# Block-sparse attention and a Sinkhorn mixture of experts on one core: how a weight's largest entry is spread over the partitions, how raw weights are loaded, and the planned order that follows

## The chip, the core and the metric

The kernel runs on one core of a Trainium2 chip. A core has five engines that run side by side, each in the order of its own program: TensorE (PE in the profile, with its weight loads as PEld), VectorE (DVE), ScalarE (ACT), GpSimd (POOL) and SyncE (SP), which here only issues DMA transfers. Matmul results lie in PSUM, in eight banks; everything else on the chip lies in SBUF, 128 partitions wide. The metric is device time of one execution in microseconds, measured on the chip. The median of three runs before the change is 2163.59 us (2163.19 to 2164.69).

## The reference

Four batches of eight heads with 768 positions and a head size of 64 go through attention with a block mask. The result is a matrix x of 3072 rows and 512 columns, which goes through eight experts. Each expert's output is weighted per row by a Sinkhorn-normalised gate. Cut to what matters:

```python
scores = np.where(mask, scale * (q @ k.T), -1e9)        # per batch and head, 768 x 768
attn = softmax(scores)
x = (attn @ v) -> 3072 x 512
P = sinkhorn(exp(x @ w_gate), 8 rounds)                 # 3072 x 8
for e in range(8):
    h = np.maximum(x @ w1[e], 0.0)                      # w1[e]: 512 x 1024
    ye = h @ w2[e]                                      # w2[e]: 1024 x 512
    out += P[:, e:e + 1] * ye
```

## The kernel before, in words

**Two phases.** The first 419 us of the profile are mostly attention, with gating beside its end. The rest is the experts: a loop over 32 steps, i = 4 e + b for expert e and batch b. Each step has a stage 1 (x times w1, then the maximum with zero) and a stage 2 (h times w2, then the weighted addition to the output).

**Products.** Both multiplications use Strassen's scheme: seven products of half-size blocks instead of eight, each f32 operand split into a high and a low f16 part, three matmuls per product. Stage 1 runs matmuls of 128x384 ("outer" products, L1580) and of 128x192 ("inner" ones, whose blocks are split once more, L1609) into five PSUM banks, p_0 to p_4. Stage 2 runs matmuls of 128x256 (L1932) into three banks, y_0 to y_2. DVE reads the p banks and combines them (L1553, L1646, L1662, L1684, L1840, L1848 and others write pair, u or h), and adds each y bank to the output sums acc (L1971, weighted by a tile named spare). A bank can be written again once DVE or ACT has read it.

**Weights.** The weights of an expert come as f32 from DRAM: `load_w` (L418, DMA at L422) brings the whole of w1[e] or w2[e], 2048 KB, into one tile r. Then the scale of that weight is worked out: eight absolute maxima on ACT (`magnitude`), one maximum over them on DVE (`whole`, L439), which leaves one number per partition in ma_w. `spread` (PE, L358) transposes that column through the identity matrix into a bank of stage 1, so that each partition sees all 128 numbers. `power` (DVE, L445 to L452) takes their maximum and turns it into a power-of-two scale sw and its inverse iw. With the scale, each of the seven blocks of the weight is split: the high part on ACT (L1334), the low part on DVE (L1339). Blocks that are sums or differences of raw blocks are made on POOL first (L1322), partly in place in the raw tile. The results are w2p_0 to w2p_6 for w2; for w1 they lie in the areas arena, attic and loft. These areas hold the blocks of x too, which are reloaded for each step (L473, L1487). From the scales of w1 and w2 the token weights of the expert are made (DVE, L1454 to L1458), the last of them named spare.

**Swap.** The w2p tiles exist once, so w2p of the next expert can be split only when stage 2 of this expert's last batch has used it. This part of the program, around the border of two experts, is called the swap below. There are seven of them, into e=1 to e=7, every 214 us or so. For e=0 the same jobs run before the first step.

**Order.** Every one of these pieces is a job of a plan (`Plan`, L129 to L288): it has an engine, an estimated duration, jobs it depends on, and for some a bank that it takes (`take`), gives back (`drop`) or holds. A list scheduler places the jobs, and the kernel pins each engine's program to that order. So a changed dependency or duration in a job moves others on all engines. DMAs on SP are jobs too; SP waits in its order before it issues each.

Of the kernel before, what the change touches and what calls it, by code (L numbers as in the profile page):

```python
# [9 lines left out]
F32 = mybir.dt.float32  # L10
# [6 lines left out]
ALU = mybir.AluOpType  # L17
# [3 lines left out]
P = 128  # L21
# [277 lines left out]
def tile_sparse_attention_moe(  # L299
# [116 lines left out]
    wr = {}  # L416

    def load_w(which, e):  # L418
        src, n, w = (w1, KD, FF) if which == 1 else (w2, KF, DM)
        t = raw.tile([P, KD * FF], F32, tag="r", name=f"r{which}_{e}")  # L420
        t = t.rearrange("p (c f) -> p c f", f=w)
        nc.sync.dma_start(out=t, in_=src[e].rearrange("(c p) f -> p c f", p=P))  # L422
        wr[which] = t

    def scale_steps(which, e, vector=nc.vector, scalar=nc.scalar):
# [27 lines left out]

        return [lambda k=k: part(k) for k in range(n)], whole, spread, power

# [137 lines left out]
    with ExitStack() as actx:  # L593
# [543 lines left out]
    def spare(n):  # L1137
# [151 lines left out]
    last_s3 = [()]  # L1289
    raw_free = [()]  # L1290
    pwe = {}

    def raw_load(which, e):
        return plan.dma(lambda: load_w(which, e), 2048, raw_free[0])

    def scale_jobs(which, e, loaded):
        cell = {}

        def make():
            cell["steps"] = scale_steps(which, e)  # L1300

        parts = []
        last = job({"-": 0.0}, make, (loaded,))
        for k in range(8):
            last = job({"ACT": 0.81}, lambda k=k: cell["steps"][0][k](), (last,))
            parts.append(last)
        whole = job({"DVE": 0.16}, lambda: cell["steps"][1](), parts)
        bk = hold("s1", ordered=False)

        def spread():  # L1310
            spread_bank[0] = lambda nm: bk.tile
            cell["steps"][2]()

        pe = job({"PE": 0.3}, spread, (whole,), take=(bk,), lag=2.0)
        power = job({"DVE": 1.2}, lambda: cell["steps"][3](), (pe,), drop=(bk,), rush=True)
        scaled[which, e] = power
        return parts, power
# [13 lines left out]
    def split_jobs(which, e, dst, src, deps):  # L1331
        s = lambda: wr["s", which]
# [4 lines left out]
        lo = job(  # L1337
            {"DVE": 1.29},
            lambda: nc.vector.scalar_tensor_tensor(  # L1339
                out=dst[:, 1], in0=src(), scalar=s(), in1=dst[:, 0], op0=ALU.mult, op1=ALU.subtract  # L1340
            ),
            (hi,), port=True,
        )
        return [hi, lo]

    def fetch_w1(e):
# [6 lines left out]

        loaded = job({"-": 0.0}, views, (loaded,) + tuple(last_s3[0]))
        parts, power = scale_jobs(1, e, loaded)
        g = lambda k: (lambda: a[k])
        q00, q10, q01, q11, s3 = (g(k) for k in ((0, 0), (1, 0), (0, 1), (1, 1), "s3"))
        base = tuple(parts)
        d_s3 = tts(s3, q00, q10, KH, base, 1.27)
        d_s1 = tts(q10, q10, q11, KH, tuple(d_s3), 1.27, ALU.add)  # L1360
        out = {}
# [5 lines left out]
        def inner(p, src, deps):  # L1367
# [36 lines left out]
        put(4, q10, d_s1)  # L1404
        last_s3[0] = tuple(out[5])
        raw_free[0] = tuple(x for p in out for x in out[p])
        split_done[1, e] = out

    def fetch_w2(e, loaded=None, done=None):
# [7 lines left out]

        if e == 0 or loaded is None:
            if loaded is None:
                loaded = raw_load(2, e)  # L1420
            start = job({"-": 0.0}, views, (loaded,) + tuple(last_s3[0]))
            parts, _ = scale_jobs(2, e, start)
# [705 lines left out]
```

## Time and profile before

| | before |
|---|---|
| median of three runs | 2163.59 us |
| profiled execution, its own time | 2163.22 us |
| its span in the profile | 2161.4 us |
| PE busy | 2113.7 us |
| DVE busy | 1778.1 us |
| ACT busy | 1363.3 us |
| POOL busy | 1170.3 us |

The span runs from the first to the last recorded instruction; the profiled execution's own time is 1.8 us longer. In the rows of the profile, "L1609 PE MATMUL p<-loft 128x192" is a matmul of line 1609 that writes a p bank from weights in loft; "x6" is a count; "[1.00 <-DVE pair L1662]" says that the engine stood idle for 1.00 us before it, until an instruction of line 1662 on DVE, which writes a tile pair, had ended. SPq is SP's queue of DMA issues.

### The profile page before, as it was taken

How to read it: one execution, taken by the hardware profiler on the slowest of the kernel's cores; microseconds unless marked ns; L12 is line 12 of the kernel's file. 1: busy time of each engine (PE TensorE's matmuls, PEld its weight loads, DVE VectorE, ACT ScalarE, POOL GpSimd, SP SyncE). 2: the span in 40 equal slices, each digit the busy share in tenths (PEclk: the TensorE clock that was granted, in tenths of full speed). 3: DMA queues.
4: the chain of work that ended last, by engine and by line, in shares of the span. 5: the costliest groups of instructions: out<-in, count | busy, mean ns of one | idle time of the engine just before them, and what ended most of it. 6: DMA issues, size and time to landing. Idle time of an engine off the chain costs nothing.

```text
span 2161.4 us, 51347 instructions
## 1 busy us (share of the span) xinstructions
PE 2113.7 (98%) x20620; PEld 1707.3 (79%) x20620; DVE 1778.1 (82%) x3240; ACT 1363.3 (63%) x2593; POOL 1170.3 (54%) x1336
## 2 busy tenths in 40 slices
PE   6999999999999999999999999999999999999999
PEld 4777776667777778788888888888888888888887
DVE  8878888688788878777988888888878987888776
ACT  4788888786567666655565556655655565556442
POOL 5556768465245547544665466446554564556323
PEclk9999999999999999999999999999999999999999
DMA  7667866432454644554354444544554445454421
GB/s 173 142 134 165 211 132 140 146 113 96 138 182 152 218 158 134 195 177 144 135 182 169 152 140 164 193 140 146 172 178 140 159 159 179 140 178 148 140 96 67
DMA packets 229412, 331.04 MB, mean 153 GB/s; under 512 B 135452, under 2 KB 153908, under 8 KB 229172
## 3 DMA queue, kind: packets, MB, share of 16 engines
q1 hardware_dynamic: 228608, 327.73, 49.6%
q8 instruction: 161, 2.64, 0.5%
q14 instruction: 79, 0.65, 0.1%
q10 hardware_dynamic: 564, 0.03, 0.0%
HBM read 228.62 MB, written 67.63 MB: 137 GB/s over the span
## 4 chain that ended last, share of the span: by engine, by line
PE 91%; DVE 6%; DMA 1%; issue 1%; ACT 1%; POOL 0%; SPq 0%; DVEq 0%; ACTq 0%; POOLq 0%
PE y L1932 39%; PE p L1580 23%; PE p L1609 15%; PE u L964 4%; PE t L902 2%; PE t L899 2%; PE m L866 2%; PE m L869 2%; DVE top L875 1%; DMA qt<-qs 1%; PE u L995 0%; DVE acc L1971 0%; DVE w2p L1339 0%; DVE pl L917 0%; DVE h L1815 0%
## 5 line engine op out<-in xcount | busy, mean ns | idle before, releaser
L1932 PE MATMUL y<-w2p,h 128*128 128x256 f16 x8064 | 969.3, 273 | 4.0 <-DVE w2p L1339 2.7
L1932 PEld LDWEIGHTS <-h 128*128 128x128 f16 x8064 | 785.4, 98 | 123.0 <-issue 3.7
L1798 POOL TENSOR_TENSOR h<-pair,h 128x384 f16<-128x384 f32 x413 | 414.7, 1016 | 489.9 <-ACT h L1809 429.7
L1971 DVE SCALAR_TENSOR_TENSOR acc<-y,spare,acc 128x256 f32<-128x256 f32 (+1 forms) x588 | 303.5, 518 | 151.5 <-PE y L1932 148.0
L1809 ACT ACTIVATE h<-pair 128x384 f16<-128x384 f32 x640 | 314.8, 516 | 138.9 <-DVE pair L1840 51.2
L1580 PE MATMUL p<-arena 128*128 128x384 f16 x1728 | 323.1, 326 | 1.4 <-DVE pair L1553 1.4
L1794 ACT ACTIVATE pair<-pair 128x384 f32<-128x384 f32 x384 | 194.9, 518 | 191.3 <-DVE pair L1553 161.8
L1553 DVE SCALAR_TENSOR_TENSOR pair<-p,pair 128x384 f32<-128x384 f32 x384 | 212.6, 555 | 93.6 <-PE p L1580 89.9
L1580 PEld LDWEIGHTS <-arena 128*128 128x128 f16 x1728 | 166.7, 98 | 83.5 <-issue 1.8
L875 DVE TENSOR_REDUCE top<-m 128x1 f32<-128x768 f32 x192 | 181.8, 951 | 48.5 <-PE m L869 47.7
L1609 PEld LDWEIGHTS <-loft 128*128 128x128 f16 x2304 | 198.8, 98 | 26.8 <-issue 11.1
L907 ACT ACTIVATE pe<-t,qk 128x768 int32<-128x768 f32 x192 | 172.3, 899 | 70.3 <-PE t L902 61.9
L1580 PE MATMUL p<-attic 128*128 128x384 f16 x1152 | 214.3, 326 | 0.0
L1840 POOL TENSOR_TENSOR pair<-pair,pair 128x384 f32<-128x384 f32 x120 | 128.3, 1076 | 106.6 <-DVE pair L1840 82.9
L1609 PE MATMUL p<-loft 128*128 128x192 f16 x1728 | 176.7, 246 | 8.5 <-DVE pair L1662 7.1
L1580 PEld LDWEIGHTS <-attic 128*128 128x128 f16 x1344 | 130.6, 98 | 66.8
L1798 POOL TENSOR_TENSOR h<-u,h 128x384 f16<-128x384 f32 x121 | 117.1, 975 | 119.4 <-ACT h L1809 77.1
L1562 ACT ACTIVATE u<-p 128x384 f32<-128x384 f32 x216 | 105.5, 488 | 103.7 <-PE p L1609 97.7
L1562 ACT ACTIVATE pair<-p 128x384 f32<-128x384 f32 x168 | 82.1, 490 | 113.0 <-PE p L1609 63.5
L1322 POOL TENSOR_TENSOR r<-r 128x256 f32<-128x256 f32 (+1 forms) x150 | 125.7, 850 | 39.2 <-DVE attic L1339 29.2
L866 PE MATMUL m<-kt,qt 128*128 128x512 f16 (+1 forms) x384 | 127.7, 333 | 10.0 <-DMA kt<-ks 6.6
L921 POOL TENSOR_SCALAR pl<-pe 128x768 f16<-128x768 uint16 x112 | 96.3, 863 | 71.7 <-ACT pe L907 69.4
(235 smaller groups left out, 3769.4 us busy)
## 6 DMA issues: line engine op xcount, KB each, us to landing
arena<-xd SPq DMA_DIRECT2D x128, 384.0 KB, 3.3
accd<-acc SPq DMA_DIRECT2D x56, 768.0 KB, 4.2
acc<-accd SPq DMA_DIRECT2D x56, 768.0 KB, 5.3
attic<-xd SPq DMA_DIRECT2D x96, 384.0 KB, 3.3
loft<-xsd SPq DMA_DIRECT2D x96, 384.0 KB, 4.9
r<-in_moe_w_dram SPq DMA_DIRECT2D x16, 2048.0 KB, 9.0
xd<-loft SPq DMA_DIRECT2D x28, 384.0 KB, 3.0
arena<-in_q_dram SPq DMA_DIRECT2D x16, 384.0 KB, 4.1
```

The costliest lines, as they stand in the source:

```text
L866: nc.tensor.matmul(sc[:, lo:hi], lhsT=qt[:, 0, c], rhs=ka[:, lo:hi], start=True, stop=False)
L875: nc.vector.tensor_reduce(out=tops[n][:, c : c + 1], in_=sc[:, :S], axis=AX.X, op=ALU.max)
L907: nc.scalar.activation(pe, sc[:, :S], AF.Exp, bias=EXP_SHIFT, scale=qk[n // 2][3])
L1553: lambda: nc.vector.scalar_tensor_tensor(out=out_(), in0=bank_(), scalar=HDOWN, in1=add(), op0=ALU.mult, op1=ALU.add),
L1562: lambda: nc.scalar.activation(out_(), bank_(), AF.Relu if relu else AF.Copy, scale=HDOWN),
L1580: nc.tensor.matmul(bk.tile[:, :TH], lhsT=w1p[p][:, l, kc, fs], rhs=xp[p][:, r, kc], start=(fresh and kc == 0 and m == 0), stop=(kc == KH - ...
L1609: nc.tensor.matmul(bk.tile[:, c * HT : (c + 1) * HT], lhsT=lhs(l, c), rhs=rhs(rr), start=(fresh and c == 0 and m == 0), stop=(m == 2), ski ...
L1794: return job({"ACT": 0.52}, lambda: nc.scalar.activation(view(), view(), AF.Relu), dep)
L1798: nc.gpsimd.tensor_tensor(out=out_, in0=x, in1=y, op=ALU.subtract)
L1809: lambda: nc.scalar.activation(h.tile[:, 0], src(), AF.Relu if relu else AF.Copy),
L1932: nc.tensor.matmul(py, lhsT=hh[i, p, kc].tile[:, l, tsl], rhs=w2p[p][:, r, kc], start=(old is None and kc == 0 and m == 0), stop=(kc == h2 ...
L1971: lambda dst=dst, src=src, t=t: nc.vector.scalar_tensor_tensor(out=dst(), in0=src(), scalar=pwe[e][:, t : t + 1] if e else 1.0, in1=dst(), ...
```

## The change

- **Scales by DMA.** For w2 of all experts and w1 of e=1 to e=7 (15 scales), the transpose `spread` and the bank it holds are gone. Two DMAs on SP take its place. The first (peak_d) stores the 128 numbers of ma_w to DRAM; the second (peaks) loads all 128 of them into every partition of an SBUF tile of 128x128, and waits for the first. `power` reads that tile. It was marked as urgent (`rush`) in the plan and no longer is. The scale of w1 for e=0, in the attention phase, keeps its transpose.
- **Raw weights in halves.** The raw tile is fixed, and each weight of e=1 to e=7 comes as two DMAs of 1024 KB, half 1 first; w1 and w2 of e=0 still come in one piece. Each waits only for the readers of its own half. The eight absolute maxima wait for their half each, half 1 first, and are no longer chained one behind the other.
- **Dependencies.** The POOL differences that only read raw blocks no longer wait for the maxima; those that write in place wait for them. The scale tiles have names per expert.
- **Order.** The scheduler deals the jobs anew. Lines below L424 move by 2 to 12.

The short title of the change also speaks of sums that are loaded, added and stored, and of w1 differences in other quadrants. In the code the sums of acc are loaded, added and stored in the same experts before and after, and the w1 differences have the same operands.

```diff
-    def load_w(which, e):
+    def load_w(which, e, half=None):
         src, n, w = (w1, KD, FF) if which == 1 else (w2, KF, DM)
-        t = raw.tile([P, KD * FF], F32, tag="r", name=f"r{which}_{e}")
-        t = t.rearrange("p (c f) -> p c f", f=w)
-        nc.sync.dma_start(out=t, in_=src[e].rearrange("(c p) f -> p c f", p=P))
+        if "raw" not in wr:
+            wr["raw"] = raw.tile([P, KD * FF], F32, name="raw_w")
+        t = wr["raw"].rearrange("p (c f) -> p c f", f=w)
+        cs = slice(0, n) if half is None else slice(half * n // 2, (half + 1) * n // 2)
+        nc.sync.dma_start(out=t[:, cs], in_=src[e].rearrange("(c p) f -> p c f", p=P)[:, cs])
         wr[which] = t
...
+    peak_d = [dram.tile([P, 1], F32, name=f"peak_d_{n}") for n in range(2)]
+    peaks = [sk.tile([P, P], F32, name=f"peaks_{n}") for n in range(2)]
...
     def raw_load(which, e):
-        return plan.dma(lambda: load_w(which, e), 2048, raw_free[0])
+        return [
+            plan.dma(lambda j=j: load_w(which, e, j), 1024, raw_free[j]) for j in (1, 0)
+        ][::-1]
...
-        for k in range(8):
-            last = job({"ACT": 0.81}, lambda k=k: cell["steps"][0][k](), (last,))
-            parts.append(last)
+        made = job({"-": 0.0}, make, (loaded[1],))
+        parts = [
+            job({"ACT": 0.81}, lambda k=k: cell["steps"][0][k](), (made, loaded[k // 4]))
+            for k in (4, 5, 6, 7, 0, 1, 2, 3)
+        ]
         whole = job({"DVE": 0.16}, lambda: cell["steps"][1](), parts)
-        bk = hold("s1", ordered=False)
-
-        def spread():
-            spread_bank[0] = lambda nm: bk.tile
-            cell["steps"][2]()
-
-        pe = job({"PE": 0.3}, spread, (whole,), take=(bk,), lag=2.0)
-        power = job({"DVE": 1.2}, lambda: cell["steps"][3](), (pe,), drop=(bk,), rush=True)
+        out_ = plan.dma(
+            lambda: nc.sync.dma_start(out=peak_d[which - 1], in_=cell["steps"][4]), 1, (whole,)
+        )
+
+        def back():
+            nc.sync.dma_start(
+                out=peaks[which - 1],
+                in_=peak_d[which - 1].rearrange("p one -> (p one)").unsqueeze(0).to_broadcast([P, P]),
+            )
+            wr["all", which] = peaks[which - 1]
+
+        in_ = plan.dma(back, 64, (out_,))
+        power = job({"DVE": 1.2}, lambda: cell["steps"][3](), (in_,))
...
         q00, q10, q01, q11, s3 = (g(k) for k in ((0, 0), (1, 0), (0, 1), (1, 1), "s3"))
-        base = tuple(parts)
-        d_s3 = tts(s3, q00, q10, KH, base, 1.27)
-        d_s1 = tts(q10, q10, q11, KH, tuple(d_s3), 1.27, ALU.add)
+        base = (seen,)
+        d_s3 = tts(s3, q00, q10, KH, (seen, loaded[0]), 1.27)
+        d_s1 = tts(q10, q10, q11, KH, tuple(d_s3) + tuple(parts), 1.27, ALU.add)
...
-        d_t1 = tts(t1, m01, m00, h2, base, 0.73)
+        d_t1 = tts(t1, m01, m00, h2, (seen, loaded[0]), 0.73)
...
-        d6 = tts(m01, m01, m11, h2, tuple(d_t1), 0.73)
+        d6 = tts(m01, m01, m11, h2, tuple(d_t1) + tuple(parts), 0.73)
```

What this does to the programs shows best at a swap. The first place is DVE's program at the swap into e=7; ma_w2_7, sw2_7 and iw2_7 are the largest entries, the scale and its inverse, pc, pcb and spare_10 the token weights, and u and pair hold sums of stage 1. Before, behind `power` and one addition to acc, it reads:

```order
L1646 SCALAR_TENSOR_TENSOR u_1_8053<-p_0_8011,pair_1_8044 128x384
L1971 SCALAR_TENSOR_TENSOR acc_2_8058<-y_1_8017,spare_9_24643,acc_2_8058 128x256
L1662 SCALAR_TENSOR_TENSOR pair_2_8045<-p_4_8015,u_0_8052 128x2x192
L1454 TENSOR_SCALAR pc_7_27366<-iw1_7_25132,iw2_7_27139 128x1
L1456 TENSOR_SCALAR pcb_7_27368<-inv_v_72,pc_7_27366 128x4
L1458 TENSOR_TENSOR spare_10_27370<-pw_73,pcb_7_27368 128x24
L1971 SCALAR_TENSOR_TENSOR acc_2_8058<-y_2_8018,spare_9_24643,acc_2_8058 128x256
L1662 SCALAR_TENSOR_TENSOR pair_8_8051<-p_4_8015,u_1_8053 128x2x192
L1339 SCALAR_TENSOR_TENSOR w2p_1_8005<-r2_7_26922,sw2_7_27138,w2p_1_8005 128x1024
```

After the change, the same engine at the same swap:

```order
L447 TENSOR_REDUCE ma_w2_7_26941<-peaks_1_8069 128x1
L448 TENSOR_SCALAR ma_w2_7_26941<-ma_w2_7_26941 128x1
L450 TENSOR_SCALAR ma_w2_7_26941<-ma_w2_7_26941 128x1
L451 RECIPROCAL sw2_7_26942<-ma_w2_7_26941 128x1
L453 TENSOR_SCALAR sw2_7_26942<-sw2_7_26942 128x1
L454 TENSOR_SCALAR iw2_7_26943<-ma_w2_7_26941 128x1
L1465 TENSOR_SCALAR pc_7_27339<-iw1_7_25291,iw2_7_26943 128x1
L1467 TENSOR_SCALAR pcb_7_27341<-inv_v_72,pc_7_27339 128x4
L1469 TENSOR_TENSOR spare_10_27343<-pw_73,pcb_7_27341 128x24
L1982 SCALAR_TENSOR_TENSOR acc_2_8057<-y_0_8015,spare_9_24589,acc_2_8057 128x256
L1859 SCALAR_TENSOR_TENSOR p_4_8014<-p_4_8014,pair_5_8047 128x384
L1351 SCALAR_TENSOR_TENSOR w2p_1_8004<-raw_w_4236,sw2_7_26942,w2p_1_8004 128x1024
```

Before, the same bank p_4 is read twice (by L1662) with the three small jobs and an addition between; after, the nine small jobs stand in one piece, no bank is read twice in that stretch, and the first low part (w2p_1) follows as the third row behind them.

The second place is PE's program at the same swap. Before, where two of stage 1's inner groups share the bank p_4:

```order
L1609 MATMUL p_4_8015<-attic_95 128x192
L1609 LDWEIGHTS attic_95
L1609 MATMUL p_4_8015<-attic_95 128x192
L1609 LDWEIGHTS loft_87
L1609 MATMUL p_4_8015<-loft_87 128x192
```

After, where stage 2 goes from the old w2p_2 to the new w2p_1 (y_2 is followed by y_0):

```order
L1943 LDWEIGHTS h_7_8025
L1943 MATMUL y_2_8017<-w2p_2_8005,h_7_8025 128x256
L1943 LDWEIGHTS h_7_8025
L1943 MATMUL y_2_8017<-w2p_2_8005,h_7_8025 128x256
L1943 LDWEIGHTS h_16_8034
L1943 MATMUL y_0_8015<-w2p_1_8004,h_16_8034 128x256
```

Before, one group follows the other in the same bank with nothing between them, 12 matmuls of y ahead and the first new w2p_1 behind both. After, 24 matmuls with w2p_2 and 36 with the new w2p_1 stand in one row, and the inner groups of stage 1 come behind them, with 18 other matmuls between two uses of one bank (p_1).

The third place is SP's program at the same swap; xd and xsd are the blocks of x and their sums in DRAM, accd the output sums in DRAM. Before:

```order
L1487 DMA loft_87<-xsd_1_8068 128x1536
L422 DMA r2_7_26922<-in_moe_w2_dram 128x8x512
L473 DMA attic_95<-xd_1_77 128x1536
L1487 DMA loft_87<-xsd_1_8068 128x1536
L473 DMA arena_91<-xd_1_77 128x1536 x2
L473 DMA attic_95<-xd_1_77 128x1536
L473 DMA arena_91<-xd_2_78 128x1536
L1487 DMA loft_87<-xsd_2_8069 128x1536
L1999 DMA accd_3_1_8066<-acc_1_8057 128x1536
```

After:

```order
L424 DMA raw_w_4236<-in_moe_w2_dram 128x4x512
L475 DMA attic_95<-xd_1_77 128x1536
L1498 DMA loft_87<-xsd_1_8071 128x1536
L475 DMA arena_91<-xd_1_77 128x1536 x2
L1316 DMA peak_d_1_8067<-ma_w2_7_26941 128x1
L1320 DMA peaks_1_8069<-peak_d_1_8067 128x128
L475 DMA attic_95<-xd_1_77 128x1536
L475 DMA arena_91<-xd_2_78 128x1536
L1498 DMA loft_87<-xsd_2_8072 128x1536
L2010 DMA accd_3_1_8065<-acc_1_8056 128x1536
```

The two small DMAs stand between the loads of x for two steps, the second right behind the first, whose end it waits for.

More of the change, by code (lines that the diff above doesn't have):

```diff
@@ L452, in power @@
             vector.tensor_scalar(inv, a, 1.0 / top, None, ALU.mult)
-        return [lambda k=k: part(k) for k in range(n)], whole, spread, power
+        return [lambda k=k: part(k) for k in range(n)], whole, spread, power, a
     KB = 1024
@@ L1072, in start_w @@
             load_w(1, 0)
-            parts, whole, spread, power = scale_steps(1, 0)
+            parts, whole, spread, power, _ = scale_steps(1, 0)
             WORK.update((part, (0.0, 0.8, 0.0)) for part in parts)
@@ L1289, in tile_sparse_attention_moe @@
     last_s3 = [()]
-    raw_free = [()]
+    raw_free = {0: (), 1: ()}
     pwe = {}
     def raw_load(which, e):
-        return plan.dma(lambda: load_w(which, e), 2048, raw_free[0])
+        return [
+            plan.dma(lambda j=j: load_w(which, e, j), 1024, raw_free[j]) for j in (1, 0)
+        ][::-1]
     def scale_jobs(which, e, loaded):
@@ L1300, in make @@
             cell["steps"] = scale_steps(which, e)
-        parts = []
-        last = job({"-": 0.0}, make, (loaded,))
-        for k in range(8):
-            last = job({"ACT": 0.81}, lambda k=k: cell["steps"][0][k](), (last,))
-            parts.append(last)
-        whole = job({"DVE": 0.16}, lambda: cell["steps"][1](), parts)
-        bk = hold("s1", ordered=False)
-        def spread():
-            spread_bank[0] = lambda nm: bk.tile
-            cell["steps"][2]()
-        pe = job({"PE": 0.3}, spread, (whole,), take=(bk,), lag=2.0)
-        power = job({"DVE": 1.2}, lambda: cell["steps"][3](), (pe,), drop=(bk,), rush=True)
+            wr["s", which, e] = wr["s", which]
+        made = job({"-": 0.0}, make, (loaded[1],))
[3 more added lines that the diff above has]
+        ]
+        whole = job({"DVE": 0.16}, lambda: cell["steps"][1](), parts)
+        out_ = plan.dma(
[9 more added lines that the diff above has]
+        power = job({"DVE": 1.2}, lambda: cell["steps"][3](), (in_,))
         scaled[which, e] = power
@@ L1331, in split_jobs @@
     def split_jobs(which, e, dst, src, deps):
-        s = lambda: wr["s", which]
+        s = lambda: wr["s", which, e]
         hi = job(
@@ L1352, in views @@
             a["s3"] = wr["s3"]
-        loaded = job({"-": 0.0}, views, (loaded,) + tuple(last_s3[0]))
+        seen = job({"-": 0.0}, views, (loaded[1],) + tuple(last_s3[0]))
         parts, power = scale_jobs(1, e, loaded)
@@ L1376, in inner @@
             part = lambda l: sums[p][:, l].rearrange("p (k i) f -> p k (i f)", k=KH)
-            s = lambda: wr["s", 1]
+            s = lambda: wr["s", 1, e]
             hi = job(
@@ L1404, in fetch_w1 @@
         put(4, q10, d_s1)
-        last_s3[0] = tuple(out[5])
-        raw_free[0] = tuple(x for p in out for x in out[p])
+        last_s3[0] = tuple(out[5]) + tuple(d_s4)
+        raw_free[0] = tuple(x for p in (0, 4, 5) for x in out[p])
+        raw_free[1] = tuple(x for p in (1, 2, 3) for x in out[p]) + tuple(d_s1)
         split_done[1, e] = out
@@ L1416, in views @@
             r["t1"] = raw.tile([P, h2, DH], F32, tag="s3", name=f"t1_{e}")
[L1418 to L1422, printed above, removed]
-        else:
-            start = job({"-": 0.0}, views, (loaded,))
-            parts = [start]
-            scaled[2, e] = start
+        if loaded is None:
+            loaded = raw_load(2, e)
+        else:
+            loaded = [loaded, loaded]
+        seen = job({"-": 0.0}, views, (loaded[1],) + tuple(last_s3[0]))
+        parts, _ = scale_jobs(2, e, loaded)
         g = lambda k: (lambda: r[k])
         m00, m10, m01, m11, t1 = (g(k) for k in ((0, 0), (1, 0), (0, 1), (1, 1), "t1"))
-        base = tuple(parts)
+        base = (seen,)
         out = {}
@@ L1447, in fetch_w2 @@
         last_s3[0] = tuple(four)
-        raw_free[0] = tuple(x for p in out for x in out[p])
+        raw_free[0] = tuple(x for p in (0, 5, 6) for x in out[p]) + tuple(d3)
+        raw_free[1] = tuple(x for p in (1, 2, 3) for x in out[p]) + tuple(d5) + tuple(d6)
         split_done[2, e] = out
```

## The prediction

> **What bounds the kernel now.** I read the page first: the busy shares and the chain of waits that ended last, whose shares are by engine.
>
> ```profile
> PE 2113.7 (98%) x20620; PEld 1707.3 (79%) x20620; DVE 1778.1 (82%) x3240; ACT 1363.3 (63%) x2593; POOL 1170.3 (54%) x1336
> PE 91%; DVE 6%; DMA 1%; issue 1%; ACT 1%; POOL 0%; SPq 0%; DVEq 0%; ACTq 0%; POOLq 0%
> ```
>
> TensorE is nearly never idle. So the change can win two things: matmul work that it removes, and idle gaps of PE. Next is the table by stage (length, then busy time and count of PE, PEld, DVE, ACT, POOL, then granted clock, DMA share and GB/s) for the expert loop.
>
> ```profile
> 419.00:2120.00 1701.00, 1685.43 (x14941) 1395.17 (x14942) 1407.90 (x2628) 1032.33 (x2132) 892.81 (x928) 1.00 0.46 153
> ```
>
> PE sat idle there for 1701.0 − 1685.4 = 15.6 us in all: the ceiling for anything that only takes waits away. The clock is full. The waits of PE from 415 us on say who ends the gaps (total, times, longest).
>
> ```profile
> PE p L1609 <- DVE pair L1662: 7.1, 6, 2.6
> PE y L1932 <- DVE w2p L1339: 2.7, 3, 1.9
> PE p L1609 <- DVE pair L1840: 1.5, 3, 0.6
> PE y L1932 <- DVE h L1815: 1.1, 2, 0.9
> ```
>
> No DMA and no POOL row stands among them. Nearly half is one wait: an inner group wants its bank back, which L1662 on DVE has yet to read. PE's timeline (start, length, what, and in brackets the idle time before it) shows where, here for the swaps into e=4 to e=7.
>
> ```profile
> 1331.20 0.66 PE L1609 MATMUL p<-attic 128*128 128x192 f16 x6
> 1332.86 0.66 PE L1609 MATMUL p<-loft 128*128 128x192 f16 x6 [1.00 <-DVE pair L1662]
> ...
> 1546.37 0.66 PE L1609 MATMUL p<-loft 128*128 128x192 f16 x6 [0.65 <-DVE pair L1662]
> 1546.86 2.78 PE L1932 MATMUL y<-w2p,h 128*128 128x256 f16 x24
> 1550.17 1.07 PE L1609 MATMUL p<-loft 128*128 128x192 f16 x11 [0.53 <-DVE pair L1840]
> ...
> 1760.43 0.66 PE L1609 MATMUL p<-loft 128*128 128x192 f16 x6 [0.71 <-DVE pair L1662]
> ...
> 1973.93 0.66 PE L1609 MATMUL p<-loft 128*128 128x192 f16 x6 [0.65 <-DVE pair L1662]
> ...
> 1975.13 0.93 PE L1932 MATMUL y<-w2p,h 128*128 128x256 f16 x7 [0.43 <-DVE w2p L1339]
> 1976.32 0.75 PE L1932 MATMUL y<-w2p,h 128*128 128x256 f16 x4 [0.27 <-DVE h L1815]
> 1977.72 1.48 PE L1609 MATMUL p<-loft 128*128 128x192 f16 x16 [0.65 <-DVE pair L1840]
> ```
>
> DVE's timeline at the first of these says why the bank came late.
>
> ```profile
> 1326.18 0.28 DVE L445 TENSOR_REDUCE ma_w<-p 128x1 f32<-128x128 f32 x1
> ...
> 1327.14 0.14 DVE L452 TENSOR_SCALAR iw<-ma_w 128x1 f32<-128x1 f32 x1
> ...
> 1327.83 0.67 DVE L1458 TENSOR_TENSOR spare<-pw,pcb 128x24 f32<-128x24 f32 x1
> ...
> 1330.60 0.54 DVE L1662 SCALAR_TENSOR_TENSOR pair<-p,u 128x384 f32<-128x384 f32 x1
> 1331.07 1.27 DVE L1339 SCALAR_TENSOR_TENSOR w2p<-r,sw,w2p 128x1024 f16<-128x1024 f32 x1
> 1332.26 0.55 DVE L1662 SCALAR_TENSOR_TENSOR pair<-p,u 128x384 f32<-128x384 f32 x1
> ```
>
> From 1326.18 to 1328.50, `power` (1.1 us) and the token weights (1.1 us) hold DVE for 2.3 us, and a low part of w2p of 1.27 us stands between two reads of the bank; PE's gap ends as the second read does. So the swap crowds DVE with urgent scale work while PE has only stage 1's inner groups, in few banks, to go on with: w2p of the new expert isn't ready.
>
> **The slots.** A row's last matmul ends late by the model: six of 128x192 begin at 1546.37, and the next row 0.49 later, so a slot is 0.082 us and the surplus 0.66 − 0.49 = 0.17. Then 128x256 takes (2.78 − 0.17)/24 = 0.109. Eight of 128x384 in the next rows give (1.46 − 0.17)/8 = 0.161, and the transpose 0.11 (from its start to the next row's).
>
> ```profile
> 440.72 0.27 PE L358 MATMUL p<-ident,ma_w 128*128 128x128 f32 x1
> 440.83 1.46 PE L1580 MATMUL p<-arena,attic 128*128 128x384 f16 x8
> ```
>
> **Part a, the transposes.** 15 go, at 0.11: −1.65 us, all on PE, the engine that sets the end.
>
> **Part b, the swaps into e=4 to e=7.** I counted PE's matmuls in the planned order between DVE's `whole` (maximum known per partition) and the first matmul with the new w2p_1. At e=7 before: 36 of 128x256, 36 of 128x192 and the transpose, 3.92 + 2.95 + 0.11 = 7.0 us; after: 57, 30 and 6 of 128x384, 6.21 + 2.46 + 0.97 = 9.6. At e=4, 5 and 6 it goes from 7.3, 7.0 and 7.0 to 14.1, 12.0 and 9.7. The scale is thus known earlier, no bank of stage 1 is held for a transpose, and groups that share a bank have other matmuls between. I take all eight gaps of the timeline above as gone: 1.00 + 0.65 + 0.53 + 0.71 + 0.65 + 0.43 + 0.27 + 0.65 = 4.9. What is late next is the first w2p_1, in part d.
>
> **Part c, e=1 to e=3.** PE's timeline has these gaps there.
>
> ```profile
> 719.22 1.03 PE L1932 MATMUL y<-w2p,h 128*128 128x256 f16 x8 [1.90 <-DVE w2p L1339]
> ...
> 841.79 0.66 PE L1609 MATMUL p<-arena,loft 128*128 128x192 f16 x6 [0.65 <-DVE pair L1684]
> ...
> 844.51 0.72 PE L1932 MATMUL y<-w2p,h 128*128 128x256 f16 x5 [0.86 <-DVE h L1815]
> ...
> 898.83 0.66 PE L1609 MATMUL p<-attic 128*128 128x192 f16 x6 [0.67 <-DVE ma_w L445]
> 902.13 1.12 PE L1609 MATMUL p<-loft 128*128 128x192 f16 x6 [2.64 <-DVE pair L1662]
> ...
> 903.79 0.58 PE L1932 MATMUL y<-w2p,h 128*128 128x256 f16 x2 [0.33 <-DVE w2p L1339]
> ...
> 1118.68 0.66 PE L1609 MATMUL p<-loft 128*128 128x192 f16 x6 [1.40 <-DVE pair L1662]
> ```
>
> At e=2 (898 to 904 us) `whole` stood only 5.0 us of PE work ahead of the first use; now 12.5. I take its 0.67 + 2.64 + 0.33 = 3.6 as gone, but the low part of w2p_1 (1.27 us) now stands 0.3 us of PE work ahead of its use, so some 1.0 comes back: −2.6. At e=1 it stands directly ahead of its use, so the 1.90 stays. The gaps at 841 and 844 lie outside a swap, and 1118's I keep: those 2.9 us are only in the low end.
>
> **Part d, the two DMA hops.** `whole`, store, load, `power` is a chain in which each link waits for the last. While DVE stands at `power`, which is in its fixed order, every read of a bank behind it waits, and then PE. Behind the load of peaks on SP wait the blocks of x and the accd stores; each block goes into an area whose next use is a step away, so a few us there cost nothing. If that cover fails, PE shows a wait for a DMA. No hop of this size is in the trace. The nearest rows (KB, median us from issue to landing; the first is a store to DRAM, the second a 16 KB load at the program's start), and, last, one issue on SP:
>
> ```profile
> xd<-loft SPq DMA_DIRECT2D x7, 384.0 KB, 2.3
> wg<-in_moe_w_gate_dram ACTq DMA_DIRECT2D x1, 16.0 KB, 3.8
> arena<-xd SPq DMA_DIRECT2D x128, 384.0 KB, 3.3
> acc<-accd SPq DMA_DIRECT2D x56, 768.0 KB, 5.3
> 1323.99 0.32 SPq L473 DMA_DIRECT2D attic<-xd  x1
> ```
>
> I take the store at 2.3 (a store to DRAM on the same queue) and the load at 3.3, with two issues of 0.3: 6.2 us. PE work between `whole` and `power`, in the planned order, is 5.5, 15.7, 8.7, 9.3, 8.2, 6.8, 5.7 and 5.7 us for e=0 to e=7: short by 0.7 at e=0 only, and by 0.5 at e=6 and e=7. There the first use is tighter still: 6.2 + `power` 1.1 + token weights 1.1 + an addition 0.5 + one read of a bank 0.5 + low part 1.27 = 10.7 against 9.6, so 1.0 each. Sum +2.7. For w1 the work between is 41 us or more (18 at e=2): nothing. Bounds: 2.3 a hop (5.2 with the issues) gives +0.2; 3.8 a hop (8.2) gives 2.7 + 1.4 + 3.1 + 3.1 = +10.3.
>
> On the price of such a hop, the Trainium skill, page "DMA: Bandwidth & Descriptors", section "Anatomy of one DMA — SWDGE (gpsimd) path", gives a fixed 2.0 us per transfer, mostly the wait until the last write is confirmed, and warns that this is surprisingly long when the target is HBM, as it is for the first hop here. By its figure the two hops with the issues would be an estimated 4.6 us and the sum 2155.6; its warning speaks against this change, and the rows above, all 2.3 or more, lean to the warning.
>
> **Part e, the new deal.** Jobs between swaps are dealt anew too. The low part of w2p_1 stands 0.9 to 3.9 us of PE work ahead of its use at e=3 to e=7, and some bank will be late somewhere. The gaps that I left in place (2.9 us outside parts b and c) are an example of the size; half of that as new ones: +1.5. Ends: 0 and +4.
>
> **At nothing.** The halves of the raw loads, the unchained maxima and the earlier differences: no PE row waits for a raw load, ACT or POOL, and ACT has 37% and POOL 46% of the span free; without that cover the first maximum would wait for a 1024 KB load. Some low parts and sums move from DVE to POOL (17 h parts, seven pair sums back); PE waits for DVE, so this can only help where POOL has room. 30 more small issues and 15 more raw ones on SP, at 0.3 us, are 14 us in 1700 on a queue that mostly waits for PE, as its longest wait shows:
>
> ```profile
> SPq L473 <- PE p L1609: 494.7, 77, 17.2
> ```
>
> The "plain form" and "other quadrants" of the title have no line of their own.
>
> **Sum.** The profiled execution took 2163.2 (span 2161.4 and 1.8 around it), 0.4 below the median. 2163.2 − 1.65 − 4.9 − 2.6 + 2.7 + 1.5 = **2158.3 us**.
>
> **The rivals.**
> - Hops of 3.8, as for the 16 KB load: +10.3 in place of +2.7, 2165.9. For it: small transfers in a busy queue, and the one small row there is. Against: that row is from another queue, in the start of the program.
> - The waits are only dealt anew, or the halves and the title's words bring nothing: five banks, and a DVE that is 83% busy in the loop (1407.9 of 1701), meet at another place; only the transposes go and the hops come: 2163.2 − 1.65 + 2.7 = 2164.3. For it: the nine small jobs of the scale still stand in one piece of DVE's program. Against: `whole` stands earlier in all.
> - **Slower:** hops of 5.3, as acc's loads, 11.2 with the issues. DVE then stands at `power` past its cover: 5.7 + 0 + 2.5 + 1.9 + 3.0 + 4.4 at e=0 to e=5 and 6.1 at e=6 and e=7, 29.7 in all: 2163.2 − 9.15 + 29.7 + 1.5 = 2185.3. It decides from about 4.0 us a hop, where part d reaches 12.4. For it: the hops share one queue with 768 KB transfers. Against: those carry 768 KB and these 64 KB at most.
>
> **How the numbers follow.** Within 0.2% (4.3 us) of the median no measurement of this kernel tells a change. Forecast 0.55 (0.46 faster by more than that, 0.09 within); hops of 3.8, 0.15 (0.13 within, 0.02 slower); dealt anew, 0.17 within; slow hops 0.13. So faster 0.46, same 0.39, slower 0.15. The low end takes the hops at +0.2, nothing for part e and the 2.9 us of part c as gone: 2163.2 − 1.65 − 4.9 − 2.6 + 0.2 − 2.9 = 2151.4, a little less for matmul records that the trace lacks: 2150.5. The high end covers the first two rivals with part e at its +4 (2165.9 + 2.5 = 2168.4): 2168.5. What lies beyond is the slower rival and a tail, under 0.2.
>
> **What would show it.** Right: no PE transposes after 419 us; the gaps behind L1662 (L1673 now) at the four last swaps gone; peak_d and peaks together under 6.5 us, and DVE's wait for peaks at `power` near zero at e=1 to e=5 and about 0.5 at e=6, e=7. Wrong: a row "DVE ma_w <- DMA peaks" of several us with PE waiting for acc, pair or w2p behind it (slow hops); a sum of PE gaps after 419 us that is still about 15 us (dealt anew); PE waiting for arena, attic or loft from a DMA (SP held up by the hop).

## The result and the profile after

| | before | after |
|---|---|---|
| median | 2163.4 us (4 runs, 2163.19 to 2164.69) | 2194.56 us (4 runs, 2192.31 to 2198.29) |
| ratio to before | | 1.0144, 95% interval 1.0127 to 1.0162 |
| profiled execution, its span | 2163.22, 2161.4 | 2194.32, 2192.5 |

The change makes the kernel 31 us slower. The forecast was 2158.3 us with a range of 2150.5 to 2168.5: the time lies outside, on the other side.

The page of the changed kernel, busy shares and the chain that ended last:

```profile
PE 2122.0 (97%) x20605; PEld 1709.9 (78%) x20605; DVE 1761.3 (80%) x3217; ACT 1364.8 (62%) x2593; POOL 1181.5 (54%) x1359
PE 86%; DVE 6%; DMA 5%; issue 1%; ACT 1%; POOL 0%; SPq 0%; DVEq 0%; ACTq 0%; POOLq 0%
PE y L1943 38%; PE p L1591 21%; PE p L1620 14%; PE u L966 4%; PE t L904 2%; PE t L901 2%; PE m L868 2%; PE m L871 2%; DMA peak_d<-ma_w 2%; DMA peaks<-peak_d 2%; DVE top L877 1%; DMA qt<-qs 1%; DVE acc L1982 0%; PE u L997 0%; DVE pl L919 0%
```

PE's share of the chain falls from 91% to 86%, and DMA's rises from 1% to 5%, all of it the two hops. DVE's waits, the waits of PE (from 415 us on), and the two hops among the DMA issues (count, KB, median us from issue to landing), with the least, median and largest landing of the store:

```profile
DVE ma_w L447 <- DMA peaks<-peak_d: 42.2, 7, 7.7
...
PE y L1943 <- DVE acc L1982: 12.3, 4, 4.6
PE y L1943 <- DVE w2p L1351: 5.2, 5, 1.4
PE p L1620 <- DVE pair L1695: 4.7, 4, 2.6
...
peaks<-peak_d SPq DMA_DIRECT2D x15, 64.0 KB, 5.5
peak_d<-ma_w SPq DMA_DIRECT2D x15, 0.5 KB, 7.9
...
DMA to landing us min/median/max: 6.9/7.9/10.9
```

DVE stands at `power` for 42.2 us in seven places, which are all the scales of w2 except e=1. The store of 0.5 KB takes 7.9 us and the load 5.5 us, where the prediction had 2.3 and 3.3. The swap into e=7 shows one such place in order of time: SP's issues, DVE, then PE (start, length; idle time in brackets).

```profile
1986.24 0.32 SPq L1316 DMA_DIRECT2D peak_d<-ma_w  x1
1993.96 0.32 SPq L1320 DMA_DIRECT2D peaks<-peak_d  x1
...
1986.07 0.15 DVE L441 TENSOR_REDUCE ma_w<-mx_w 128x1 f32<-128x8 f32 x1
...
1991.90 0.48 DVE L1982 SCALAR_TENSOR_TENSOR acc<-y,spare,acc 128x256 f32<-128x256 f32 x1 [0.20 <-PE y L1943]
2000.12 0.28 DVE L447 TENSOR_REDUCE ma_w<-peaks 128x1 f32<-128x128 f32 x1 [7.73 <-DMA peaks<-peak_d]
...
1994.99 2.78 PE L1943 MATMUL y<-w2p,h 128*128 128x256 f16 x24
2002.41 0.40 PE L1943 MATMUL y<-w2p,h 128*128 128x256 f16 x1 [4.64 <-DVE acc L1982]
2004.07 7.45 PE L1943 MATMUL y<-w2p,h 128*128 128x256 f16 x47 [1.26 <-DVE w2p L1351]
```

The maxima are known at 1986.22, the load goes out 7.74 us later, and `power` starts 13.9 us after the maxima. DVE has work for 6 us of that. PE has work until 1997.8; then a y bank and the new w2p_1 hang on DVE, and PE is idle for 4.64 and 1.26 us. And the 47 matmuls behind the gap take (7.45 − 0.17)/47 = 0.155 us each instead of 0.109. Short windows of the same place show why (length, PE busy and count, granted clock, DMA share, GB/s):

```profile
1990.00:1998.00 8.00, 7.77 (x76) 1.00 0.03 5
1998.00:2002.00 4.00, 0.00 (x0) 0.96 0.83 330
2002.00:2008.00 6.00, 4.33 (x20) 0.50 0.61 228
2008.00:2012.00 4.00, 4.00 (x38) 0.94 0.99 349
```

After the idle stretch the granted clock is 0.50 for 6 us and more. So such a wait is paid a second time, in slow matmuls. The pages of both kernels split the loss. PE's idle time goes from 2161.4 − 2113.7 = 47.7 to 2192.5 − 2122.0 = 70.5 us, +22.8. Its busy time grows by 8.3 us, although 15 transposes, some 1.65 us by the prediction's count, are gone: about 10 us of slower matmuls. Idle and busy time together make 31.1 us, the difference of the spans.

### The profile page after: what moved, and what is told of

It reads as the page before. It is cut to its first block, busy times and chain, and to the rows that moved or that the text cites. A ratio compares the mean times of both kernels' runs of the same rounds, so it can differ in the third digit from the quotient of the medians.

```text
span 2192.5 us, 51495 instructions
## 1 busy us (share of the span) xinstructions
PE 2122.0 (97%) x20605; PEld 1709.9 (78%) x20605; DVE 1761.3 (80%) x3217; ACT 1364.8 (62%) x2593; POOL 1181.5 (54%) x1359
## 3 DMA queue, kind: packets, MB, share of 16 engines
q8 instruction: 161, 2.64, 0.5%
## 4 chain that ended last, share of the span: by engine, by line
PE 86%; DVE 6%; DMA 5%; issue 1%; ACT 1%; POOL 0%; SPq 0%; DVEq 0%; ACTq 0%; POOLq 0%
PE y L1943 38%; PE p L1591 21%; PE p L1620 14%; PE u L966 4%; PE t L904 2%; PE t L901 2%; PE m L868 2%; PE m L871 2%; DMA peak_d<-ma_w 2%; DMA peaks<-peak_d 2%; DVE top L877 1%; DMA qt<-qs 1%; DVE acc L1982 0%; PE u L997 0%; DVE pl L919 0%
## 5 line engine op out<-in xcount | busy, mean ns | idle before, releaser
L1943 PE MATMUL y<-w2p,h 128*128 128x256 f16 x8064 | 973.9, 274 | 20.6 <-DVE acc L1982 12.3
L1809 POOL TENSOR_TENSOR h<-pair,h 128x384 f16<-128x384 f32 x430 | 428.2, 1007 | 495.8 <-ACT h L1820 434.7
L1809 POOL TENSOR_TENSOR h<-u,h 128x384 f16<-128x384 f32 x116 | 106.6, 925 | 101.6 <-ACT h L1820 90.7
L1334 POOL TENSOR_TENSOR raw_w<-raw_w 128x256 f32<-128x256 f32 (+1 forms) x150 | 121.5, 819 | 58.9 <-DVE attic L1351 27.6
```

What stands on the lines that cost most here:

```text
L1809: nc.gpsimd.tensor_tensor(out=out_, in0=x, in1=y, op=ALU.subtract)
L1943: nc.tensor.matmul(py, lhsT=hh[i, p, kc].tile[:, l, tsl], rhs=w2p[p][:, r, kc], start=(old is None and kc == 0 and m == 0), stop=(kc == h2 ...
```

## The experiments

The theory after the result: the hops are the whole loss, because they take 13 us where the plan covers them with 6 to 9 us. The rival: the halves, the changed dependencies or the new deal cost time themselves. Ratios are to the kernel before, measured beside each, with 95% intervals; its median there was 2164.8 to 2165.6 us.

**Experiment 1, the transpose back.** Everything else of the change stays.

```diff
-        out_ = plan.dma(
-            lambda: nc.sync.dma_start(out=peak_d[which - 1], in_=cell["steps"][4]), 1, (whole,)
-        )
...
-        in_ = plan.dma(back, 64, (out_,))
-        power = job({"DVE": 1.2}, lambda: cell["steps"][3](), (in_,))
+        pe = job({"PE": 0.3}, spread, (whole,), take=(bk,), lag=2.0)
+        power = job({"DVE": 1.2}, lambda: cell["steps"][3](), (pe,), drop=(bk,), rush=True)
```

> The changed kernel with the PE transpose in place of the two DMAs; halves, new dependencies and a plan dealt anew stay. Theory 1 (the hops are the whole loss: store and load together take 13 us, the plan covers them with 6 to 9 us, DVE stands still behind them, PE runs dry and then runs at half clock): at or below the kernel before, 2156 to 2164 us, no granted clock under 0.9 for more than one swap. Theory 2 (halves, changed dependencies and the new deal cost time themselves): 2170 to 2190 us.

Measured: 2157.18 us, ratio 0.9962 (0.9949 to 0.9976). Theory 1 holds: without the hops the rest of the change is faster than the kernel before. PE's longest rows of waits are now:

```profile
PE p L1615 <- DVE pair L1668: 2.9, 3, 1.6
PE y L1938 <- DVE w2p L1346: 2.5, 1, 2.5
PE y L1938 <- DVE h L1821: 2.1, 3, 1.0
```

L1668 is the combined read that was L1662 before, there with 7.1 us in six places.

**Experiment 2, the hops alone.** The kernel before, with the same two DMAs for the transpose.

> The kernel before with the two DMAs in place of the transpose and nothing else. Theory 1: PE work between the partition maxima and the scale is 5.5, 20.2, 12.7, 10.7, 7.2, 7.2, 7.2 and 7.4 us for w2 of e=0 to 7, against 13.3 us for the hops: DVE waits for peaks 7.8 + 0 + 0.6 + 2.6 + 6.1 + 6.1 + 6.1 + 5.9 = 35 us, and the time goes up by 20 to 32 us, to 2183 to 2195. Theory 2: up by less than 10 us.

Measured: 2208.45 us, ratio 1.0199 (1.0185 to 1.0213), 43 us slower and so beyond what was expected. DVE's wait for peaks was a little more than counted (40.4 against 35 us), but PE loses more than in the changed kernel. Its rows of waits say where: the first group that stands behind the hop is here one of stage 1 that wants its bank back (the first row is DVE's, the second PE's):

```profile
DVE ma_w L445 <- DMA peaks<-peak_d: 40.4, 6, 8.2
...
PE p L1616 <- DVE pair L1669: 34.8, 6, 8.3
```

**Experiment 3, the plan told.** The hops stay, and the planner counts them with their measured length.

```diff
-                j.end = dma_free + self.DMA_LAND
+                j.end = dma_free + self.DMA_LAND + j.late
...
+        out_.late, in_.late = 5.9, 3.4
```

> The changed kernel, hops and all, but the planner counts 7.9 us for the store and 5.7 us for the load (2.0 and 2.3 before). PE work between maxima and scale is then 14.4 us or more at every w2. Theory 1: DVE's wait for peaks under 3 us in all, no half clock at a swap, 2156 to 2168 us. Theory 2 (the hops also delay loads, or the deal itself is worse): 2172 us or more.

Measured: 2166.76 us, ratio 1.0008 (0.9999 to 1.0017). DVE no longer waits for peaks at all, and 28 of the 31 us are gone. But 9.6 us to experiment 1 remain, near the upper end of what theory 1 allowed: the scale stands 15 us or more of PE work behind the maxima (3 to 5 us in experiment 1), and the waits behind combined reads and low parts come back in its place:

```profile
PE p L1621 <- DVE pair L1696: 7.6, 9, 2.0
PE y L1944 <- DVE w2p L1352: 4.0, 4, 1.1
```

**Why is the store slow? Experiments 4, 7 and 10** put probe stores on SP at the scales of w1, where some 40 us are spare. In experiment 4 they stand ahead of the store of peak_d:

```diff
+        def store():
+            if which == 1 and e in (1, 4, 6):
+                nc.sync.dma_start(out=pad_d[0][:, 0:1], in_=cell["steps"][4])
+            if which == 1 and e in (2, 5, 7):
+                nc.sync.dma_start(out=pad_d[1], in_=wide)
+            nc.sync.dma_start(out=peak_d[which - 1], in_=cell["steps"][4])
```

> The changed kernel; ahead of the store of 128 packed numbers, the scale of w1 at e=1, 4, 6 also stores them to rows 512 B apart (4 B each), and at e=2, 5, 7 stores 128 whole rows of 512 B from a tile that DVE fills. Packed stores took 6.9 to 10.9 us from issue to landing. If 4 B writes that share a DRAM line are what is slow: rows apart about 3 us, whole rows about 3 us. If any 4 B write is slow: rows apart 7 us, whole rows 3 us. If it is the queue or the receipt whatever the shape: all three 7 us.

Measured, among the DMA issues:

```profile
peak_d<-ma_w SPq DMA_DIRECT2D x14, 0.5 KB, 8.5
pad_d<-wide SPq DMA_DIRECT2D x3, 64.0 KB, 9.7
pad_d<-ma_w SPq DMA_DIRECT2D x3, 0.5 KB, 7.1
```

All are slow, which reads like "whatever the shape". That reading was wrong, as the next two show: the probes had the packed store right behind them. In experiment 7 the probes stand behind the load of peaks, with no packed store near.

```diff
             wr["all", which] = peaks[which - 1]
+            if which == 1 and e in (1, 5):
+                nc.sync.dma_start(out=probe_d[e][:, 0:1], in_=ident[:, 0:1])
+            if which == 1 and e in (2, 6):
+                nc.sync.dma_start(out=probe_d[e][:, 0:64], in_=ident[:, 0:64])
...
```

> The changed kernel with a probe store to DRAM behind the load of peaks of w1, nobody waiting for it: 128 packets of 4 B in rows 512 B apart (e=1, 5), of 256 B (e=2, 6), of 512 B (e=3, 7), of 768 B (e=4). Experiment 4 had the small packed store right behind its probes, which could have held them back. If packets of 512 B and below are slow to be confirmed: 768 B lands in 2.5 to 3 us, 512 B and below in 6 us or more. If only those below 512 B: 512 B lands in 3 us too. If it was the neighbour alone: all land in 2.5 to 3.5 us.

Measured: 4 B in rows 512 B apart landed in 4.5 and 4.4 us; 256 B in 6.4 and 3.7; 512 B in 3.8 and 4.9; 768 B in 3.8. They queue behind the load of peaks, so a part of each is that wait: the 6.4 stands behind a load that took 6.1 itself. Here neither the size nor the number of packets makes a store slow. Experiment 10 changes the place alone: 128 packets of 4 B each time, packed, 32 B apart, or 512 B apart.

```diff
+            if which == 1:
+                step = {1: 1, 4: 1, 7: 1, 2: 8, 5: 8, 3: 128, 6: 128}[e]
+                rows = probe_d[e].rearrange("a b -> (a b)")[0 : P * step].rearrange("(p s) -> p s", s=step)
+                nc.sync.dma_start(out=rows[:, 0:1], in_=ident[:, 0:1])
```

> The changed kernel with a probe store of 128 packets of 4 B from a tile that was written long before, behind the load of peaks of w1, nobody waiting for it: packed into 512 B (e=1, 4, 7), 32 B apart (e=2, 5), 512 B apart (e=3, 6; experiment 7 had 4.4 us for these, behind the load's packets). If packets to one stretch are served one after the other: packed 7 us or more, 512 B apart 4 to 4.5 us, 32 B apart between. If it is the fresh source or the wait ahead: all three 4 to 4.5 us.

Measured: packed 10.3, 7.9 and 8.9 us; 32 B apart 6.9 and 4.0; 512 B apart 3.7 and 3.7. The rows of the second packed probe (e=4) and of the second one 512 B apart (e=6), each with its neighbour in the queue:

```profile
peaks<-peak_d SPq DMA_DIRECT2D x1, 64.0 KB, 3.8
probe_d<-ident SPq DMA_DIRECT2D x1, 0.5 KB, 7.9
```

```profile
peaks<-peak_d SPq DMA_DIRECT2D x1, 64.0 KB, 3.9
probe_d<-ident SPq DMA_DIRECT2D x1, 0.5 KB, 3.7
```

The neighbours, the data and the source are alike; the addresses differ, and the swap. All three packed probes are slow, behind loads of 3.8 to 4.6 us, and both that lie 512 B apart are not. The 6.9 us of the first probe 32 B apart isn't such a cost, for its neighbour took 7.2. In this pair, 128 writes packed into one stretch of 512 B cost 4.2 us more than the same writes in rows of their own, an estimated 33 ns for each if they go one by one. The time passes behind the moves: in the changed kernel at e=7 the last of the store's 128 packets moved 1.8 us after the issue, the landing came 7.7 us after it, and between them the DMA engines had next to nothing to do (a share of 0.03):

```profile
1988.10:1993.96 5.86, 5.86 (x57) 1.00 0.03 3
```

What in the memory path does this was not looked into.

**Experiment 8, the load.** A probe load behind the load of peaks, of 128 different rows or of one row for all partitions.

```diff
+            if which == 1 and e in (1, 4, 6):
+                nc.sync.dma_start(out=probe, in_=w1[0][0:P, 0:P])
+            if which == 1 and e in (2, 5, 7):
+                nc.sync.dma_start(out=probe, in_=w1[0][0:1, 0:P].to_broadcast([P, P]))
```

> The changed kernel with a probe load of 128 packets of 512 B behind the load of peaks of w1, nobody waiting for it: 128 different rows (e=1, 4, 6) or one row for all partitions (e=2, 5, 7). peaks takes 3.7 to 7.3 us, 5.5 in the median. If reading one line 128 times is slow: different rows 3.0 to 3.5 us, one row 5 us or more. If it is the size of the packets or their place in a busy queue: both about 5 us.

Measured: different rows 4.2, 3.7 and 3.6 us, one row 5.7 and 5.3 (the third has no landing in the trace). But peaks itself, always one row, took 4.4, 3.9 and 3.8 beside the first three and 5.8 and 5.5 beside the others: each probe lands as its neighbour does, so the place in the queue sets the time. A cost of the one row isn't shown.

**Experiment 9, four packets.** DVE turns the 128 numbers in blocks of 32, and four packets of 128 B go to the same 512 B of DRAM. The load, and the plan, stay: PE's program is row for row that of the changed kernel, and DVE's has 15 rows more.

```diff
-            lambda: nc.sync.dma_start(out=peak_d[which - 1], in_=cell["steps"][4]), 1, (whole,)
...
+        def top():
+            cell["steps"][1]()
+            nc.vector.transpose(turn, cell["steps"][4].to_broadcast([P, 32]))
...
+            nc.sync.dma_start(
+                out=peak_d[which - 1].rearrange("(k f) one -> k (f one)", f=32), in_=turn[0:P:32],
+            )
```

> The changed kernel, but DVE first turns the 128 numbers in blocks of 32, so that the store has 4 packets of 128 B in place of 128 packets of 4 B; the load and the plan stay. If the 128 writes to one 512 B stretch are served one after the other (the packets were moved 1 us after the issue, the store was confirmed 5.4 us after that): the store lands in 2 to 3 us, the two hops take 7.5 to 8.5 us, DVE's wait for peaks falls from 42 to about 12 us, and the time to 2165 to 2172 us. If it is the confirmation of any small or fresh store: 7 to 8 us again, and 2190 to 2196 us.

Measured: 2152.40 us, ratio 0.9942 (0.9925 to 0.9959). That is 42 us faster than the changed kernel, and better than either theory had it. The swap into e=7 on SP and DVE, and the busy shares of its page:

```profile
1952.75 0.51 SPq L1320 DMA_DIRECT2D peak_d<-turn  x1
1954.30 0.32 SPq L1328 DMA_DIRECT2D peaks<-peak_d  x1
...
1958.15 0.48 DVE L1990 SCALAR_TENSOR_TENSOR acc<-y,spare,acc 128x256 f32<-128x256 f32 x1 [0.20 <-PE y L1951]
1958.56 0.28 DVE L447 TENSOR_REDUCE ma_w<-peaks 128x1 f32<-128x128 f32 x1
...
PE 2109.7 (98%) x20605; PEld 1705.0 (79%) x20605; DVE 1767.1 (82%) x3232; ACT 1364.8 (63%) x2593; POOL 1186.3 (55%) x1359
```

The load goes out 1.55 us after the store's issue, where it was 7.72, and `power` follows its neighbour on DVE without a wait, 4.26 us after the load's issue. The load is faster too, at this place by 1.8 us or more (it took 6.1 in the changed kernel); why wasn't tried apart, so the 42 us are not all the store's. With the same PE program, idle time falls by 70.5 − (2150.4 − 2109.7) = 29.8 us and busy time by 12.3 us. So 12 of the 42 us were the same matmuls taking longer; behind the attention phase the granted clock never drops in this trace, while in the changed kernel it drops six times.

**Experiment 11** is the same kernel again.

> Experiment 9 once more, in more rounds, beside the kernel before and experiment 12 on one chip. If its gain is real: 2150.5 to 2154 us and 0.9935 to 0.9955 of the kernel before. If part of it was the chip: above 2156 us.

Measured: 2154.26 us, ratio 0.9955 (0.9941 to 0.9969). The gain over the kernel before holds, a little over the expected times. The profiled execution (2158.43 us) had one wait of 4.33 us that experiment 9 had not, of which more at the end.

**Where does the gain come from? Experiments 5, 6 and 12.** Experiment 5 is experiment 1 with each raw weight in one piece again; experiment 6 is experiment 1 with the old dependencies of the differences.

```diff
-        return [
-            plan.dma(lambda j=j: load_w(which, e, j), 1024, raw_free[j]) for j in (1, 0)
-        ][::-1]
+        j = plan.dma(lambda: load_w(which, e), 2048, raw_free[0] + raw_free[1])
+        return [j, j]
```

> Experiment 1 (transpose back, 2157.2 us) with each raw weight loaded in one piece again, the changed dependencies kept. If the halves are what brings the gain: the maxima end later, PE work from them to the first use of w2p_1 falls from 10 to 14 us back to 6.3 to 6.9 us at e=2 to e=7, the gaps behind the combined reads return, 2163 to 2167 us. If it is the earlier differences or luck of the deal: within 1.5 us of 2157.

> Experiment 1 with the old dependencies of the POOL differences and splits (all wait for all eight maxima), halves kept. PE work from the maxima to the first use of w2p_1 stays at 10 us or more. If the halves bring the gain: 2156 to 2160 us. If the earlier differences bring it: 2162 us or more.

Measured: experiment 5 2164.92 us, ratio 1.0000 (0.9991 to 1.0009): the whole gain is gone, and the waits behind combined reads and low parts are back:

```profile
PE p L1614 <- DVE pair L1667: 4.6, 4, 2.4
PE y L1937 <- DVE w2p L1345: 4.1, 5, 1.8
```

Experiment 6 took 2161.55 us, ratio 0.9988 (0.9978 to 0.9998), between its two answers: halves with the old dependencies keep a third (by the ratios) to a half (by the medians) of the gain, and a new wait of 3.5 us has come in (PE p L1586 behind DVE pair L1846). So the gain needs the halves, and half of it or more needs also the earlier differences or the deal that they allow; these two weren't separated.

Experiment 12 is experiment 2 with the four packets: short hops, raw weights in one piece, old dependencies.

> Experiment 2 (the kernel before with the hops alone; raw weights in one piece, old dependencies) with the store of four packets. The hops take 6 to 8.5 us as in experiment 9; PE work from the maxima to the scale is 7.2 us and to the first use of w2p_1 8.5 us at e=4 to e=7. If the hops, once short, are neutral and the gain comes from the halves, which let the maxima end earlier: the first use is late by 1.5 to 2.5 us at these four swaps, 2160 to 2168 us. If the hops themselves bring the gain (no transpose, no bank held): 2150 to 2156 us as in experiment 9.

Measured: 2167.02 us, ratio 1.0008 (0.9999 to 1.0018). DVE never waits for peaks, `power` starts 6.4 to 6.8 us after the maxima at e=4 to e=7, and yet nothing is won:

```profile
PE p L1624 <- DVE pair L1699: 4.7, 4, 2.5
PE y L1947 <- DVE w2p L1354: 4.3, 6, 0.8
PE p L1624 <- DVE pair L1677: 4.0, 6, 0.8
```

So short hops bring nothing by themselves, and the gain of experiments 1, 9 and 11 needs the halves. Each of these kernels is one deal of the scheduler; how far the time moves by the deal alone wasn't measured.

## Why the prediction was wrong

**The step that failed is part d, the price of the hops.** It took the store at 2.3 us "(a store to DRAM on the same queue)" and the load at 3.3, from rows of 384 KB; measured, 7.9 and 5.5, and 13.0 to 14.1 us from the maxima to `power` where DVE waited, with 14.5 at e=4, where the store was issued 0.8 us late. The bounds, 2.3 to 3.8 us a hop, reasoned from size: smaller, so not slower. What decided for the store was that 128 packets go to one stretch of 512 B (experiments 9 and 10); why the load took 5.5 us and not 3.3 stays open, but probes right behind it landed as late as it did (experiment 8). No row of before showed a store of that form. The Trainium skill, page "DMA: Bandwidth & Descriptors", section "Anatomy of one DMA — SWDGE (gpsimd) path", has a fixed 2.0 us per transfer, for DMAs issued from GpSimd. The store of four packets, issued from SP, is near it (the load that waits for it goes out 1.55 to 1.98 us after its issue at six of the eight scales of w2), the packed one is not. The Trainium skill's warning there of late confirmation for HBM points the right way, but a store of 384 KB to the same memory landed in 2.3 us.

**The slower rival was the right mechanism at too low a price.** Its sign came: DVE waits for peaks, and PE for acc, w2p and pair behind it. It had DVE stand at `power` past its cover, decided from 4.0 us a hop, and gave 2185.3 us at 5.3. With the measured hops of 13.4 us in all, its own sum of shortfalls is 7.9 + 0 + 4.7 + 4.1 + 5.2 + 6.6 + 8.3 + 8.3 = 45.1 us, that is 2163.2 − 9.15 + 45.1 + 1.5 = 2200.7, against 2194.6. That it comes so close is in part luck: the sum takes every us of DVE's wait for one of PE and has no slow matmuls, and these two errors offset each other. Its argument against, "these 64 KB at most", was the same mistake.

**The slow matmuls behind a gap were missing** from every case: about 10 us of the 31 (12.3 of 42 against experiment 9). The prediction took "The clock is full" from a mean over 1701 us and priced a gap at its length. A short window of the same trace, behind the gap of 2.64 us at e=2, would have shown it:

```profile
902.00:904.00 2.00, 1.54 (x9) 0.50 0.47 101
```


**Parts a, b, c and e were about right in sum.** Without part d, the sum was 2155.6 us, 7.6 below the kernel before; experiment 9, in which DVE never waits for the hops, is 13.2 us below it by the medians and its repeat 10.5. By the pages, PE's idle time in experiment 9 is 40.7 us against 47.7, 7.0 less where parts b, c and e make 6.0 less; its busy time is 4.0 less where part a has 1.65. Some of the rest is the half clock at e=2 before, which experiment 9 does not have. Its trace has no PE gap over 0.5 us at the swaps into e=4 to e=7: the eight gaps of part b are gone. At e=3, whose 1.40 us were kept, 0.67 are left. At e=1, whose 1.90 were kept, 0.63 are left, but a new gap of 1.47 us stands 3.8 us ahead of them, so nothing is won there. "No bank of stage 1 is held for a transpose", one reason in part b, isn't needed for most of the gain: experiment 1 holds it again and gains 7.7 us by the medians, against 13.2 and 10.5 in experiments 9 and 11. The reason that carries is that the scale is known earlier.

**"At nothing": the halves and the earlier differences.** They were costed at nothing, and indeed no row of PE waits for a raw load in the changed kernel (POOL does once, for 11.5 us). But through the maxima the halves are what puts `whole` earlier, and so part b hangs on them (experiments 5 and 12); for half of the gain or more it hangs also on the earlier differences or their deal (experiment 6). The prediction saw the effect in the order and not its cause.

**The rival "only dealt anew"** has fallen for the version with the transpose or the short store. A wait of PE on arena, attic or loft for a DMA, named as a sign of SP held up by the hop, doesn't appear.

## What to carry to other kernels

A small transfer isn't bounded by a large one: look at how many packets go to one stretch of memory, and when numbers lie one per partition, gather them in a few rows before they are stored. Put the measured length of a new chain into the planner before judging its order, and see which engine stands in order behind its end. Price a PE gap of a few microseconds at more than its length. Here the version to keep is that of experiment 9: halves, and scales spread by a store of four packets, 0.9942 and 0.9955 of the kernel before.

## What the runs showed of the hardware

**Writes to one stretch.** 128 packets of 4 B packed into 512 B of DRAM: 7.9 to 10.3 us to landing; in rows 512 B apart, 3.7 (experiment 10). A store ahead of such a one in the queue landed late as well (experiment 4 against 7: 7.1 against 4.4 us for the same rows). Its source was also just written, where experiment 7 had an old one; these weren't separated.

**The clock after a wait.** In the changed kernel, from 435 us on, the granted clock fell to 0.50 behind PE waits of 2.94 us (at 452 us), 2.27 and 1.28 (e=2), 2.58 (e=3), 4.17 (e=4), 3.77 and 1.37 (e=6) and 4.64 (e=7), but stayed at 1.00 behind one of 3.34 us (e=5). It was low for 3.41 us each time, at e=7 for 6.83. So the length of the wait alone doesn't decide. In the trace's clock record the six drops lie 134, 62, 65, 129 and 64 times 3.413 us apart, so the clock changes at fixed steps. The next rows cut the wait at e=5 at such steps, first in the changed kernel, then in experiment 8, where PE waited only 3.02 us at the same swap:

```profile
1557.95:1561.36 3.41, 1.71 (x17) 1.00 0.42 151
1561.36:1564.77 3.41, 1.58 (x13) 1.00 0.91 372
...
1550.15:1553.56 3.41, 1.12 (x11) 1.00 0.54 205
1553.56:1556.97 3.41, 2.68 (x13) 0.50 0.95 387
1556.97:1560.38 3.41, 3.41 (x35) 1.00 0.02 4
```

The longer wait lies across the border of two steps, which have 1.7 and 1.8 us of idle time, and the clock stays. The shorter one has 2.3 us in one step, and the next step runs at 0.50. In the expert loops of all these runs (from 435 us on) a step at full clock with 2.0 us of idle time or more was followed by half clock, and one with less than 1.95 was not. The Trainium skill, page "TensorE: Matmul & The Clock Gate", section "Part 1: The HAM clock gate (the "warmup" mystery)", has the clock halved after an idle window of some 3.4 us and restored after a busy one, with windows that run freely. The traces agree in the length of the windows and in that a wait is cut by them wherever they fall; but a window that is idle for 2.0 of its 3.4 us was enough here.

**DVE kept out by POOL.** In the profile of experiment 11 a low part that takes 1.27 us lasted 6.40, and PE waited 4.33 us for it. POOL had no gap in that time, and the low part ended 1.08 us after POOL's last:

```profile
1975.23 6.40 DVE L1359 SCALAR_TENSOR_TENSOR w2p<-raw_w,sw,w2p 128x1024 f16<-128x1024 f32 x1
...
1974.24 1.80 POOL L1817 TENSOR_TENSOR h<-pair,h 128x384 f16<-128x384 f32 x2
1975.98 1.96 POOL L1859 TENSOR_TENSOR pair<-pair,pair 128x384 f32<-128x384 f32 x2
1977.90 2.65 POOL L1817 TENSOR_TENSOR h<-pair,h 128x384 f16<-128x384 f32 x3
```

It reads as if DVE's instruction got no turn until POOL paused. It is the only low part of more than 2.2 us in all the runs kept here, and no experiment was made on it.
